# A planned order for sparse attention with a gated expert: ten instead of 21 products on zeros ahead of the first scores, and a newly searched order with other numbers in its planner

## The chip, the cores and the metric

The kernel runs on one core of a Trainium2 chip. The metric is the device time of one execution in microseconds (us). A core has a matrix engine (TensorE, PE in the profile, its weight loads PEld), three engines for elementwise work (VectorE or DVE, ScalarE or ACT, GpSimd or POOL), a queue that issues the loads and stores here (SyncE, SP), and 16 DMA engines that carry them.

## The reference

Four batches, eight heads, 768 positions, head width 64. Attention looks at a band of 31 positions around each query and at 24 block summaries (the maximum of 32 keys, the mean of 32 values); a gated two-layer network with a token shift follows.

```python
    k_sum = k.reshape(B, H, nb, block, D).max(axis=3)
    v_sum = v.reshape(B, H, nb, block, D).mean(axis=3)
    ...
    scores_l_m = np.where(mask_l, scores_l, -1000000000.0)
    scores_all = np.concatenate([scores_l_m, scores_s], axis=-1)
    ...
    a = a / (np.sum(a, axis=-1, keepdims=True) + 1e-09)
    return np.matmul(a, v_all).astype(np.float32)
    ...
    xk = mu_k * x + (1.0 - mu_k) * x_prev
    xr = mu_r * x + (1.0 - mu_r) * x_prev
    k = np.maximum(xk @ w_k, 0.0)
    v = k * k @ w_v
    r = 1.0 / (1.0 + np.exp(-(xr @ w_r)))
    return (r * v).astype(np.float32)
```

## The kernel before

**The work.** A set is one batch and one pair of heads (16 sets); a unit is one half of a set's positions (32 units). The keys of a set lie in a tile `kt` in 12 windows of 64 positions, each followed by 24 columns for the block maxima, which DVE reduces (L423 to L431, tiles `kg`, `ks`) and copies in (L435). The values of a unit lie in a tile `vx`, 120 rows for each window, of which 24 are block means: for the first batch PE makes these (L447, then L455), ACT takes them out of PSUM, and POOL or DVE spreads them (L461); for the others DVE sums blocks (L381), PE transposes them (L384), and a DMA broadcasts them into each `vx` tile (L468). A unit is a chain over four engines: scores on PE (L487, tile `sc`), mask and row minimum on DVE (L497), exponentials on ACT (L501), the reciprocal of their sums (L509), a normalization on ACT, DVE or POOL (L518, L512, L523), three transposes for each head on PE (L535), copies out of PSUM (L541 on ACT, L543 on DVE, tile `pts`), products with the values on PE (L550, tile `av`), and a copy to the features (L564, L565).

Each half batch of 384 positions then goes through the network. The shifted mixes of x (L583 to L596, or on PE with diagonal matrices, L614 to L620) are split into a high and a low part, so that three fast products replace an exact one. The gate is L637 to L639 and a sigmoid (L651), the first layer L666 with relu, square and split (L672 to L681), the second layer L691, and its last eighth L717, after which DVE multiplies by the gate (L723) and SP stores. The weights come as 64-bit words and are turned into 32-bit halves by DVE, ACT and POOL (L325 to L361) in the first 100 us.

**The order.** All these operations are recorded first, with what they read and write (`Plan.op`), and nothing is decided by arrival: `ORDER` is a list of operation numbers, some with a letter for the engine, and `Plan.schedule` walks through it. It gives each operation a start in a planned time from `LENGTH` (its duration), `SWITCH` (changes of kind on PE), `LATENCY` (from an engine to a waiting one), and the `DMA_` numbers, and hands out the buffers of each pool, the one that is free first. Then the instructions are emitted in that order, and every engine runs its own queue strictly in it. So the numbers don't act on the chip; what acts is the order, the buffer that each operation gets, and the number of products on zeros.

**Products on zeros.** Until the first gate product, each gap that the plan shows on PE is filled at L764 with products of a tile `still` of zeros, one for each `WARM` = 230 ns of planned gap. They run in PE's queue like any other instruction: what stands behind them waits for them.

The line numbers are those of this kernel; in the changed one they are one or two higher from L155 on.

## Time and profile before

| what | value |
|---|---|
| median of three timed runs | 452.86 us (451.57 to 452.99) |
| the profiled execution's own time | 453.34 us |
| its span, first to last instruction | 451.5 us |
| busy: PE, DVE, ACT, POOL | 443.9, 295.9, 284.2, 45.9 us |
| chain of waits: PE, DVE, ACT, DMA | 76%, 9%, 8%, 3% |
| products on zeros (L764) | 61 in the program, 122 rows of the trace |

A row of the timeline has the start, the time until the last instruction of the row ends, the engine, the line, the operation, the tiles as written<-read, their sizes and the count; in brackets the idle time ahead of it and what ended it. An exact product of 32-bit numbers is two rows on PE. A PE row's duration runs on beyond the start of the next one, since matmuls are pipelined; the time that PE spends on one is read from start to start. A wait is put down to what came last.

### The profile page before, as it was taken

The numbers are of one execution on the slowest core, as the hardware profiler recorded it, in microseconds if no ns is written. First come the engines' busy times: TensorE is split into PE (matmuls) and PEld (weight loads), VectorE is DVE, ScalarE is ACT, GpSimd is POOL, SyncE is SP. The second block draws the span as 40 slices with busy tenths as digits, with TensorE's granted clock in tenths as the row PEclk, the third lists the DMA queues.
The fourth block names the chain that finished last, engine by engine and source line by source line (L and its number), as shares of the span: only waits on it lengthen the run. The fifth ranks groups of instructions, "written<-read, shape, count | busy, mean of one in ns | idle before, by whom it ended". The sixth has DMA issues, their size and how long they took to land.

```text
span 451.5 us, 9681 instructions
## 1 busy us (share of the span) xinstructions
PE 443.9 (98%) x3608; PEld 381.6 (85%) x3608; DVE 295.9 (66%) x944; ACT 284.2 (63%) x843; POOL 45.9 (10%) x96
## 2 busy tenths in 40 slices
PE   9999999999999999999999999999999999999996
PEld 8867888789888789888988879888889888989985
DVE  2999999997887877828677676358364533445131
ACT  2889999987775849569574586466675434232211
POOL 0443222000230100000200001011002000000000
PEclk9999999999999999999999999999999999999999
DMA  8976684551557543240723112105100000003002
GB/s 311 403 262 221 208 326 131 179 208 33 145 169 217 220 132 91 85 147 1 221 73 120 53 56 84 43 19 177 48 2 0 2 0 1 0 1 116 1 0 93
DMA packets 26878, 51.95 MB, mean 115 GB/s; under 512 B 2512, under 2 KB 14416, under 8 KB 26832
## 3 DMA queue, kind: packets, MB, share of 16 engines
q1 hardware_dynamic: 26832, 51.35, 33.8%
q8 instruction: 28, 0.46, 0.4%
q14 instruction: 18, 0.15, 0.1%
HBM read 43.28 MB, written 6.29 MB: 110 GB/s over the span
## 4 chain that ended last, share of the span: by engine, by line
PE 76%; DVE 9%; ACT 8%; DMA 3%; issue 2%; SPq 1%; DVEq 0%; POOL 0%; POOLq 0%
PE mm L666 25%; PE mm L691 23%; PE av L550 4%; PE pt L535 4%; PE mm L637 4%; PE mm L639 4%; PE mm L638 4%; PE sc L487 4%; PE mm L717 3%; DMA kt<-in_k 2%; ACT y L501 2%; PE av L764 2%; DMA vx<-vm 1%; DVE y L497 1%; DVE we L336 1%
## 5 line engine op out<-in xcount | busy, mean ns | idle before, releaser
L666 PE MATMUL mm<-xs,wk_h 128*128 128x384 f32 x512 | 101.4, 340 | 0.0
L501 ACT ACTIVATE y<-y,mn 128x120 f32<-128x120 f32 x192 | 74.1, 388 | 30.5 <-DVE mn L497 30.1
L666 PEld LDWEIGHTS mm<-xs,wk_h 128*128 128x128 f32 x512 | 89.6, 188 | 3.7 <-ACT r L672 0.8
L691 PE MATMUL mm<-wv_h,kh 128*128 128x512 f32 x168 | 67.5, 402 | 0.0
L691 PE MATMUL mm<-wv_l,kh 128*128 128x512 f32 x168 | 66.3, 395 | 0.0
L497 DVE CUSTOM_DVE_ANT_0 y<-sc,fixed_sb 128x120 f32<-128x120 f32 x192 | 46.5, 276 | 25.5 <-PE pt L535 13.3
L666 PE MATMUL mm<-xs,wk_l 128*128 128x384 f32 x256 | 55.2, 337 | 0.0
L676 ACT ACTIVATE r<-r 128x384 f32<-128x384 f32 x64 | 32.9, 521 | 27.7 <-DVE r L674 27.2
L691 PE MATMUL mm<-wv_h,kl 128*128 128x512 f32 x168 | 49.1, 401 | 0.5 <-DVE kl L681 0.5
L681 DVE TENSOR_TENSOR kl<-r,kh 128x384 fp32r<-128x384 f32 x64 | 35.3, 556 | 19.1 <-ACT kh L680 11.1
L666 PEld LDWEIGHTS mm<-xs,wk_l 128*128 128x128 f32 x256 | 45.5, 188 | 0.0
L672 ACT ACTIVATE r<-mm 128x384 f32<-128x384 f32 x39 | 19.1, 489 | 38.8 <-PE mm L666 31.0
L590 DVE SCALAR_TENSOR_TENSOR xa<-vx,fixed_sb,xa 128x384 f32<-128x384 f32 x60 | 37.0, 622 | 9.1 <-ACT xa L583 7.4
L637 PE MATMUL mm<-wr_h,xs 128*128 128x512 f32 x96 | 39.0, 407 | 0.0
L639 PE MATMUL mm<-wr_h,xs 128*128 128x512 f32 x96 | 38.0, 396 | 0.0
L638 PE MATMUL mm<-wr_l,xs 128*128 128x512 f32 x96 | 37.9, 395 | 0.0
L596 DVE TENSOR_TENSOR xs<-xa,xs 128x384 fp32r<-128x384 f32 x60 | 33.0, 558 | 6.9 <-ACT xs L593 5.6
L691 PEld LDWEIGHTS mm<-wv_h,kh 128*128 128x128 f32 x168 | 31.6, 188 | 6.5 <-ACT kh L680 0.4
L691 PEld LDWEIGHTS mm<-wv_l,kh 128*128 128x128 f32 x168 | 31.6, 188 | 6.0
L501 ACT ACTIVATION_READ_ACCUMULATOR y<-y,mn 128x1 f32 x192 | 36.5, 190 | 0.0
L691 PEld LDWEIGHTS mm<-wv_h,kl 128*128 128x128 f32 x168 | 30.7, 188 | 6.8 <-DVE kl L681 0.9
L535 PE MATMUL pt<-fixed_sb,y 128*120 128x128 f32 x192 | 33.1, 281 | 0.1
(88 smaller groups left out, 699.2 us busy)
## 6 DMA issues: line engine op xcount, KB each, us to landing
vx<-in_v SPq DMA_DIRECT2D x32, 384.0 KB, 4.1
kt<-in_k SPq DMA_DIRECT2D x15, 544.0 KB, 4.9
qt<-in_q SPq DMA_DIRECT2D x32, 192.0 KB, 3.8
out<-z SPq DMA_DIRECT2D x23, 256.0 KB, 4.2
st<-in_vT SPq DMA_DIRECT2D x12, 384.0 KB, 4.5
st<-in_w_k SPq DMA_DIRECT2D x8, 512.0 KB
st<-in_w_v SPq DMA_DIRECT2D x8, 512.0 KB
st<-in_w_r SPq DMA_DIRECT2D x4, 512.0 KB, 8.0
```

The lines of the kernel that those rows point to most:

```text
L497: op("DVE", "mask", lambda h=h, i=i, var=var: nc.vector.tensor_tensor_reduce(out=y[h].t[:, i, :], in0=sc[h].t[:, i, 0:NK], in1=mask_sb[:, ...
L501: op("ACT", "exp", lambda h=h, i=i: nc.scalar.activation(y[h].t[:, i, :], y[h].t[:, i, :], AF.Exp, bias=mn[h].t[:, i:i + 1], scale=-1.0, a ...
L535: nc.tensor.transpose(out=pt.t[0:NK, i * P:(i + 1) * P], in_=y[h].t[:, i, :], identity=ident_sb)
L590: op("DVE", "mixd", lambda xt=xt, xa=xa, p=p: nc.vector.scalar_tensor_tensor(out=xa.t, in0=xt.t[:, 1 + lo:1 + lo + HT], scalar=mu_sb[:, wh ...
L596: op("DVE", "sub", lambda xa=xa, xh=xh, xl=xl: nc.vector.tensor_tensor(out=xl.t, in0=xa.t, in1=xh.t.bitcast(F32), op=ALU.subtract), reads= ...
L637: nc.tensor.matmul(ps[t].t, xh.t[:, ts], wr_h[:, p, :], start=(p == 0), stop=False)
L638: nc.tensor.matmul(ps[t].t, xh.t[:, ts], wr_l[:, p, :], start=False, stop=False)
L639: nc.tensor.matmul(ps[t].t, xl.t[:, ts], wr_h[:, p, :], start=False, stop=(p == NPAIR - 1))
L666: nc.tensor.matmul(ps.t[:, 0:HT], w[:, j, p, :], x[p][s].t, start=(n == 0), stop=(n == 11))
L676: op("ACT", "square", lambda: nc.scalar.activation(r.t, r.t, AF.Square), reads=[(r, 0)], writes=[(r, 0)])
L681: op("DVE", "sub", lambda: nc.vector.tensor_tensor(out=kl.t, in0=r.t, in1=kh.t.bitcast(F32), op=ALU.subtract), reads=[(r, 0), (kh, 0)], wr ...
L691: nc.tensor.matmul(acc[t].t, a.t[:, t * P:(t + 1) * P], w[:, j, :], start=start, stop=stop)
```

## The change

The diff does four things. The planner's numbers are replaced: other lengths on PE, other switches and latencies, and for loads of the later batches a later landing (`LATE`, twice that for keys) and for the broadcasts of block means four times the size and 480 ns more for the issue. `ORDER` is a new list. The products on zeros are counted from 1000 ns of planned time instead of 600 and at 430 ns each up to 6000 ns, 230 ns after that. The branch for `SPLIT` isn't taken in either kernel.

```diff
-    score=776, transpose=245, vtrans=82, vpool=800, vsel=75, values=848, mixe=1400, gate=2780, gate_p=2085, e1=2085,
-    e2a=1390, e2b=695, e2=695, e2h=350,
+    score=776, transpose=245, vtrans=30, vpool=800, vsel=320, values=848, mixe=1400, gate=2797, gate_p=2095, e1=2095,
+    e2a=1398, e2b=700, e2=700, e2h=350,
...
-SWITCH = dict(MS=100, SM=112, MV=108, VM=112, TM=85, ST=55, VT=55, TS=175, TV=175)
-LATENCY = dict(M=201, S=265, V=236, T=228, DVE=115, ACT=133, POOL=180, SP=0)
+SWITCH = dict(MS=100, SM=112, MV=108, TM=55, TS=175, TV=175)
+LATENCY = dict(M=201, S=130, V=120, T=300, DVE=115, ACT=133, POOL=180, SP=0)
...
-WARM = 230
+WARM, WARM_COLD, COLD = 230, 430, 6000
...
+LATE = 400
...
 ORDER = """
-252 227 17 18 204 0 10 39 52 21 229 32 22 23 24 25 20 19 205 59 41 40 206 212 1 210 208 216 213 207 5D 211 4D 12D 214
...
+17 18 204 0 10 39 52 21 229 22 23 32 20 19 24 25 252 205 59 40 41 1 216 214 208 206 8 212 217 7 207 12D 13 210 254 79
...
-                now[e] = start + DMA_ISSUE
+                now[e] = start + DMA_ISSUE + o.more[0]
                 dma = max(dma, start + DMA_START) + DMA_EACH + o.size / DMA_BYTES_PER_NS
-                o.finish = dma + DMA_END
+                o.finish = dma + DMA_END + o.more[1]
...
-               writes=[(vt, 0)], size=P * S * 4)
+               writes=[(vt, 0)], size=P * S * 4, more=(0, LATE))
...
-               writes=[(kt, f"k{n}")], size=P * (hi - lo) * 4)
+               writes=[(kt, f"k{n}")], size=P * (hi - lo) * 4, more=(0, 2 * LATE if b else 0))
...
-                   writes=[(vw[hf], x) for x in "abc"], size=P * HW * 512)
+                   writes=[(vw[hf], x) for x in "abc"], size=P * HW * 512, more=(0, LATE if b else 0))
...
-                   reads=[(means, 0)], writes=[(x, "b")], size=NS * HW * 512)
+                   reads=[(means, 0)], writes=[(x, "b")], size=4 * NS * HW * 512, more=(480, 0))
...
-           writes=[(qt, 0)], size=P * HT * 4)
+           writes=[(qt, 0)], size=P * HT * 4, more=(0, LATE if b else 0))
...
-    end, early = 600, True
+    end, early = 1000, True
     for o in order:
         if o.eng == "PE" and early:
-            for _ in range(int((o.start - end) // WARM)):
+            for _ in range(int(max(0, o.start - max(end, COLD)) // WARM + max(0, min(o.start, COLD) - end) // WARM_COLD)):
                 nc.tensor.matmul(spare, still, still, start=True, stop=True)
```

What the new list and the new buffers do is seen in the order of the instructions on each engine. First PE from its first instruction: products on zeros (from `still`), the scores of the first and second unit (from `kt_61` and `kt_62`), and the first transposes (from `y`). Before:

```order
L764 MATMUL av_146<-still 128x128 x21
L487 MATMUL sc_143<-kt_61,qt_65 64x120 x2
L487 MATMUL sc_144<-kt_61,qt_65 64x120 x2
...
L764 MATMUL av_146<-still 128x128 x25
L487 MATMUL sc_143<-kt_62,qt_66 64x120 x2
...
L535 MATMUL pt_145<-fixed_sb,y_89 120x128 x3
L764 MATMUL av_146<-still 128x128 x3
L535 MATMUL pt_145<-fixed_sb,y_90 120x128 x3
L764 MATMUL av_146<-still 128x128 x3
L447 MATMUL mm_147<-vx_71,fixed_sb 32x128 x2
```

And in the change:

```order
L766 MATMUL av_146<-still 128x128 x10
L489 MATMUL sc_143<-kt_61,qt_65 64x120 x2
L489 MATMUL sc_144<-kt_61,qt_65 64x120 x2
...
L766 MATMUL av_146<-still 128x128 x22
L489 MATMUL sc_144<-kt_62,qt_66 64x120 x2
...
L766 MATMUL av_146<-still 128x128 x4
L537 MATMUL pt_145<-fixed_sb,y_90 120x128 x3
L766 MATMUL av_146<-still 128x128 x6
L449 MATMUL mm_147<-vx_69,fixed_sb 32x128 x2
```

The products on zeros ahead of the first scores go from 21 to 10, those ahead of the second from 25 to 22; four new ones stand ahead of the first transposes, and of these those of the other head come first. The pooling of values (from `vx`, `fixed_sb`) moves ahead of the second three transposes. In all there are 50 instead of 61.

Next DVE, from the conversion of the first gate weights (`we`, `wc`, `wr_l`, from the staging tiles `st`) to the block maxima of the second set (`kg_79`, `ks_81`, copied into `kt_62`). Before:

```order
L336 SCALAR_TENSOR_TENSOR we_139<-st_136,we_139 128x512
L298 TENSOR_SCALAR diag_sb<-fixed_sb 128x128
L340 SCALAR_TENSOR_TENSOR wc_141<-wc_141,we_139 128x512
L509 RECIPROCAL rc_100<-sm_97 128x6
L427 TENSOR_REDUCE kg_79<-kt_62 128x1
L423 TENSOR_REDUCE kg_79<-kt_62 128x48
L431 TENSOR_TENSOR ks_81<-kg_79 128x24
L332 TENSOR_SCALAR we_140<-st_137 128x512
L435 COPY kt_62<-ks_81 128x12x24
L336 SCALAR_TENSOR_TENSOR we_140<-st_137,we_140 128x512
L361 TENSOR_TENSOR wr_l<-wc_141,wr_h 128x512
```

And in the change:

```order
L341 SCALAR_TENSOR_TENSOR wc_141<-wc_141,we_139 128x512
L425 TENSOR_REDUCE kg_79<-kt_62 128x48
L429 TENSOR_REDUCE kg_79<-kt_62 128x1
L433 TENSOR_TENSOR ks_81<-kg_79 128x24
L511 RECIPROCAL rc_100<-sm_97 128x6
L437 COPY kt_62<-ks_81 128x12x24
L333 TENSOR_SCALAR we_140<-st_137 128x512
L299 TENSOR_SCALAR diag_sb<-fixed_sb,om_sb 128x128
L362 TENSOR_TENSOR wr_l<-wc_141,wr_h 128x512
L299 TENSOR_SCALAR diag_sb<-fixed_sb,om_sb 128x128
L499 ISA y_91,mn_95<-sc_143,fixed_sb 128x120
```

The copy into `kt_62` now comes ahead of the second sign (`we_140`), the reduction ahead of the reciprocal, and the diagonals (`diag_sb`) come behind all of it.

Last PE at the second transpose of block sums (from `vs`). Before, with the end of the products with values ahead of it and the gate behind it:

```order
L550 MATMUL av_146<-pts_103,vx_73 64x64
L550 MATMUL av_146<-pts_104,vx_73 64x64
L384 MATMUL pt_145<-fixed_sb,vs_82 96x128
L637 MATMUL mm_147<-wr_h,xs_116 128x512
L638 MATMUL mm_147<-wr_l,xs_116 128x512
```

And in the change, with the gate's twelve products of one row of positions cut to their ends:

```order
L552 MATMUL av_146<-pts_103,vx_72 64x64
L552 MATMUL av_146<-pts_104,vx_72 64x64
L639 MATMUL mm_149<-wr_h,xs_114 128x512
...
L641 MATMUL mm_149<-wr_h,xs_121 128x512
L385 MATMUL pt_145<-fixed_sb,vs_82 96x128
L639 MATMUL mm_147<-wr_h,xs_114 128x512
L640 MATMUL mm_147<-wr_l,xs_114 128x512
```

The transpose of `vs` stands twelve gate products further back. Counted over the whole program, PE has the same products but those on zeros; DVE has 11 more relus (36, from 25) and 8 more copies of transposed weights (26, from 18), and POOL 12 fewer normalizing rows (18, from 30) and 8 fewer mixing rows (6, from 14).

## The prediction

> **What bounds the kernel now.** I read the page's first part, then the table of windows with cuts at the places where the program changes character, then the timeline of TensorE (PE) from the start, and at last the waits of PE.

> ```profile
> span 451.5 us, 9681 instructions
> PE 443.9 (98%) x3608; PEld 381.6 (85%) x3608; DVE 295.9 (66%) x944; ACT 284.2 (63%) x843; POOL 45.9 (10%) x96
> ...
> 0.00:10.00 10.00, 9.01 (x70) 8.73 (x71) 2.00 (x8) 1.28 (x1) 0.48 (x7) 1.00 0.83 298
> 10.00:24.80 14.80, 14.26 (x187) 12.50 (x185) 14.72 (x53) 12.56 (x49) 4.91 (x6) 1.00 1.03 402
> 24.80:64.00 39.20, 39.14 (x452) 30.94 (x452) 37.60 (x129) 38.17 (x122) 13.95 (x20) 1.00 0.72 242
> 64.00:105.00 41.00, 40.95 (x279) 34.23 (x278) 39.65 (x102) 38.44 (x105) 3.55 (x6) 1.00 0.49 171
> 105.00:165.00 60.00, 58.00 (x616) 49.23 (x616) 47.90 (x182) 40.80 (x152) 10.22 (x27) 1.00 0.48 153
> 165.00:447.60 282.60, 282.52 (x2014) 245.95 (x2012) 153.31 (x473) 152.95 (x417) 12.76 (x31) 1.00 0.19 59
> ```

> The windows' columns are the stretch, its length, the busy time of PE, of its weight loads, of VectorE (DVE), ScalarE (ACT) and GpSimd (POOL), the granted clock, the DMA share and GB/s. PE is busy without a break from 24.8 to 105 us (0.11 us idle in 80.2) and from 165 to 447.6 us (0.08 us). Its work there is the same set of products before and after, so a new order can't shorten it. What can change is what PE does before 24.8 us, where much of its busy time is products on zeros that fill waits, and the 2.0 us that it is idle between 105 and 165 us. The timeline of PE shows the first part:

> ```profile
> 0.99 7.85 PE L764 MATMUL av<-still 128*128 128x128 f32 x42 [0.99 <-POOL still L758]
> 8.78 0.85 PE L487 MATMUL sc<-kt,qt 64*64 64x120 f32 x24
> 9.55 5.85 PE L764 MATMUL av<-still 128*128 128x128 f32 x50
> 15.33 0.85 PE L487 MATMUL sc<-kt,qt 64*64 64x120 f32 x24
> ...
> 24.38 0.49 PE L764 MATMUL av<-still 128*128 128x128 f32 x2 [0.54 <-DVE vx L564]
> 24.80 0.40 PE L455 MATMUL mm<-sp,fixed_sb 128*24 128x128 f32 x2
> ```

> One product on zeros in the source is two rows of the trace (21 are x42). The first 42 take 7.79 us to the first scores (0.99 to 8.78), the next 50 take 5.78 us (9.55 to 15.33). Counted in windows of line L764 alone, the early ones are slow and the later ones fast:

> ```profile
> 1.00:4.00 3.00, 3.00 (x14) 3.00 (x15) 1.00 0.70 226
> 7.00:8.00 1.00, 1.00 (x10) 1.00 (x10) 1.00 1.02 406
> ```

> 14 in 3 us are 0.214 us a row, so 0.43 us a product while slow; 50 in 5.78 us are 0.231 us a product when fast. The column of the granted clock says 1.00 in both, so the pace is the better witness. The pace turns at about 7.0 us: 7.79 us for 42 rows is 28 rows at 0.214 and 14 at 0.128. That is 6.0 us after PE's first product.

> **Products ahead of the first scores: 21 become 10.** Were they what the first scores waited for? DVE says yes:

> ```profile
> 3.60 1.25 DVE L423 TENSOR_REDUCE kg<-kt 128x24 f32<-128x384 f32 x2 [3.60 <-DMA kt<-in_k]
> ...
> 5.17 0.31 DVE L435 COPY kt<-ks 128x288 f32<-128x288 f32 x1
> 9.68 0.28 DVE L497 CUSTOM_DVE_ANT_0 y<-sc,fixed_sb 128x120 f32<-128x120 f32 x1 [4.20 <-PE sc L487]
> ...
> 10.77 0.29 DVE L298 TENSOR_SCALAR diag_sb<-fixed_sb 128x128 f32<-128x128 f32 x1
> 10.97 0.28 DVE L298 TENSOR_SCALAR diag_sb<-fixed_sb,om_sb 128x128 f32<-128x128 f32 x1
> 11.17 0.42 DVE L332 TENSOR_SCALAR we<-st 128x512 f32<-128x512 f32 x1
> ...
> 14.93 0.30 DVE L435 COPY kt<-ks 128x288 f32<-128x288 f32 x1
> ```

> The keys were complete at 5.48 us and DVE stood idle for 4.20 us until the scores came. The other operand, the queries, is issued at 1.6 us and takes 4.5 us to land:

> ```profile
> L476 SPq DMA_DIRECT2D qt<-in_q x1: 432/432/432, 1.6 to 1.6; - x1
> ...
> DMA to landing us min/median/max: 4.5/4.5/4.5
> ```

> So the first scores can't start before about 6.2 us whatever PE does; the order of the first 25 loads is the same in both kernels. In the change ten products end at 0.99 + 20 x 0.214 and a little for the first, 5.4 us. PE then pauses for 0.9 us, a wait for the queries in place of the removed products, and the scores run from 6.3 us, 2.5 us earlier than 8.78. They take 0.77 us at the fast pace (8.78 to 9.55) and, scaled by 0.43/0.231, 1.4 us at the slow one.

> **What the pause does to the pace decides the rest.** Behind the first scores stand 22 products instead of 25, and the second scores are queued behind them on PE. If the pause changes nothing and the pace turns at 7.0 us, the scores end at 7.5 us and the 22 take 5.1 us: second scores at 12.6 us. If the 6.0 us are counted anew from 6.3 us, the pace turns at 12.3 us: scores to 7.7 us, 10.7 slow products, 11.3 fast ones, second scores at 14.9 us. Before, they started at 15.33 us, so the lead is 2.7 or 0.4 us. No row shows a pause ahead of the turn. I take the middle, 1.5 us, keep both ends, and treat each as a rival; what speaks for the middle is that the pause falls in the second half of the only run-up that the trace shows.

> [...]

> Are the second scores' operands there by then? From the first mask to the end of the copy of the keys' maxima DVE took 5.55 us (9.68 to 15.23). In the change three diagonals (0.20 us each from start to start), the second sign (0.42) and the coefficients (about 0.1) stand elsewhere, so some 4.4 us. With the first mask at 7.8 to 8.0 us the operands are ready at about 12.4 us: just in time for the fast end, early for the slow one. So the products set the lead, not the data.

> Between the second scores and row 24.80 the change has 18 products instead of 15 (+0.7 us), and the 0.54 us wait at 24.38 us should go, since what it waits for is DVE's, which is ahead too. **Term one: 1.5 - 0.7 + 0.5 = 1.3 us of lead at 24.8 us**, ends 0.2 and 2.5 us.

> **Does the lead last?** From 24.8 to 105 us PE never waits, but DVE is busy for 77.25 of 80.2 us and ACT for 76.61, so they only just keep ahead. They start about 1.8 us earlier too (7.9 against 9.68 us), which covers the lead. After 165 us they have half of their time free. I keep the lead whole.

> **The idle time between 105 and 165 us.** PE's timeline shows where it waited and what ended that, in brackets, and the chain of waits what lay behind (its last two rows):

> ```profile
> 123.66 0.92 PE L550 MATMUL av<-pts,vx 120*64 120x64 f32 x24 [0.40 <-DMA vx<-vm]
> ...
> 143.74 0.91 PE L550 MATMUL av<-pts,vx 120*64 120x64 f32 x22 [0.57 <-DVE pts L543]
> ...
> 147.79 0.96 PE L691 MATMUL mm<-wv_h,kl 128*128 128x512 f32 x3 [0.51 <-DVE kl L681]
> ...
> 160.78 0.31 PE L384 MATMUL pt<-fixed_sb,vs 128*96 128x128 f32 x1 [0.53 <-DVE vs L381]
> ...
> 119.23 4.38 DMA vx<-vm
> ...
> 136.09 5.21 DMA kt<-in_k
> ```

> These four are the whole 2.0 us. One is a broadcast of block means that lands 4.4 us after its issue; the next two, at 143 and 147 us, follow a load of keys that lands after 5.2 us and stops DVE; the last is the block sums of a later batch. The new numbers put all of these loads later in the plan (0.4 us, for keys 0.8 us, for the means four times the bytes), so the order leaves them more room; and on PE the second block-mean transpose stands twelve gate products (12 x 0.23 = 2.8 us) further back, five times its wait. In the place of these waits others can come late, since SP's queue of loads is in a new order too from its 26th load on, and each load there stands behind one that waits for a buffer. Bounds: all 2.0 us go, or 2.0 us stay. **Term two: 1.3 us**, nearer the first, since three of four have a cause that the numbers now contain.

> **Changes of kind on PE.** The order counts 29 instead of 17 steps from a 512- or 384-wide product to scores or values, and 1 instead of 14 from a transpose to these.

> ```profile
> 95.75 0.40 PE L639 MATMUL mm<-wr_h,xs 128*128 128x512 f32 x1
> 96.08 0.85 PE L487 MATMUL sc<-kt,qt 64*64 64x120 f32 x24
> 96.85 0.54 PE L535 MATMUL pt<-fixed_sb,y 128*120 128x128 f32 x3
> 97.15 1.63 PE L666 MATMUL mm<-xs,wk_h 128*128 128x384 f32 x8
> ...
> 122.00 0.49 PE L535 MATMUL pt<-fixed_sb,y 128*120 128x128 f32 x3
> 122.42 0.85 PE L487 MATMUL sc<-kt,qt 64*64 64x120 f32 x24
> ```

> A product ahead of scores holds PE 0.33 us instead of 0.23 (12 x 0.1 = +1.2 us); three transposes hold it 0.42 us ahead of scores and 0.30 us ahead of a product (13 x 0.12 = -1.5 us, of which the first product behind gives some back). I cost this at nothing. The tail behind 447.6 us has the same instructions.

> **The sum.** 1.3 + 1.3 = 2.6 us off the profiled execution, whose own time is 453.34 us: 450.7 us. That execution lies 0.48 us above the median of the three timed runs (452.86), so I forecast 450.3 us for the median.

> **Rivals.** A measurement of this kernel can tell about 0.3%, 1.36 us, from no change.
> First, the pace turns on time: the lead is 2.5 us, with term two 3.8 us, 449.1 us; with all of term two 448.4 us. For it speaks that the pause is short beside 6.0 us.
> Second, the 6.0 us start anew behind the pause: lead 0.2 us, total 1.5 us, 451.4 us.
> Third, the loads come late at other places and term two is nothing: 1.3 us, 451.6 us. For it speaks that a plan whose times were thought to fit left 2.0 us before.
> Fourth, the lead is hidden anyway: operands of a later step (values, the third scores) are as late as before, and PE waits where it ran products: 452.7 us. Against it: DVE is busy for 14.72 of 14.80 us up to 24.8 us, and starts earlier.
> Fifth, **slower: DVE becomes the bound between 24.8 and 105 us.** The groups give its means:

> ```profile
> L423 DVE TENSOR_REDUCE kg<-kt 128x48 f32<-128x768 f32 x15 | 14.1, 944 | 3.0 <-DMA kt<-in_k 3.0
> L512 DVE TENSOR_TENSOR y<-y,rc 128x360 f32<-128x360 f32 x29 | 15.1, 528 | 0.2
> L543 DVE COPY pts<-pt 120x384 f32<-120x384 f32 x18 | 10.0, 553 | 7.0 <-PE pt L535 7.0
> ```

> Up to its third multiplication by the gate (L723, the end of the first half batch) the order gives DVE 15 more rows: one more reduction of keys (0.94), two normalizations (1.06), two copies of transposed weights (1.11), four masks (0.20 each from start to start), and four casts, a relu and two small ones (some 2.4 by the means of their groups), less two evacuations, a spread of means, a diagonal and a sign (some 2.4): about 3.9 us. It starts 1.8 us earlier and has 2.95 us without work there. If the free time lies where it can't be used, DVE is 2.1 us late, the lead is lost and PE waits: 453.34 + 2.1, less 0.48, 455.0 us. It decides once the added work exceeds the earlier start by more than the usable free time. Against it: the masks and the reduction are for a later batch and nothing on PE needs them yet.

> **How the numbers follow.** Forecast 0.38, pace on time 0.24, pace anew 0.10, term two nothing 0.14, hidden 0.05, DVE bound 0.09. The range takes in the first four: 447.5 (all of both terms, with 0.9 us for the scatter of 1.4 us in the three runs) to 452.9 us. Faster by over 0.3% (under 451.5): nearly all of the forecast, all of the first rival, half of the next two, 0.72; slower by over 0.3% (above 454.2): 0.08; within it 0.20.

> **What would show it.** In the profile of the change: first scores at 6.3 us with a wait of some 0.9 us ahead of them on the queries; the rows of the 22 products turning from 0.214 to 0.116 us each near 7 or 10 or 12 us; second scores at 12.6 to 14.9 us; the second selection of block means (L455 before) at about 23.5 us; PE idle under 1 us between 105 and 165 us. Wrong would be first scores later than 7 us, a PE idle time over 2 us after 25 us, or waits of PE for DVE at 25 to 105 us.

## The result, and the profile after

| what | before | change |
|---|---|---|
| median | 452.39 us (451.57 to 452.99, four runs) | 449.19 us (448.20 to 449.64, four runs) |
| ratio to before, 95% interval | | 0.9928 (0.9908 to 0.9949) |
| profiled execution's own time, span | 453.34, 451.5 us | 448.20, 446.4 us |
| span behind the second selection of block means | 426.7 us | 424.5 us |

The change is faster by 3.2 us, 0.7%. The two profiled executions are 5.14 us apart, more than the medians: the one of before lies 0.95 us above its median, the one of the change 0.99 us below. Both matter for the reading below.

The page of the change has the same share of busy time on PE, and more work on DVE in place of POOL:

```profile
span 446.4 us, 9628 instructions
PE 439.6 (98%) x3586; PEld 376.1 (84%) x3586; DVE 302.0 (68%) x968; ACT 280.7 (63%) x840; POOL 33.3 (7%) x71
```

The windows of the change, with the same columns as before's and the last cut where PE's work ends now:

```profile
0.00:10.00 10.00, 7.83 (x72) 7.52 (x73) 4.12 (x19) 3.30 (x9) 0.44 (x6) 1.00 0.81 285
10.00:24.80 14.80, 14.18 (x198) 11.45 (x197) 13.63 (x54) 13.62 (x53) 5.02 (x8) 1.00 1.03 404
24.80:64.00 39.20, 39.02 (x430) 30.92 (x430) 38.20 (x127) 38.86 (x123) 10.98 (x19) 1.00 0.70 238
64.00:105.00 41.00, 41.00 (x309) 34.57 (x308) 39.67 (x103) 37.12 (x103) 4.40 (x7) 1.00 0.57 189
105.00:165.00 60.00, 60.00 (x608) 50.98 (x607) 51.04 (x197) 47.64 (x169) 3.80 (x9) 1.00 0.57 177
165.00:442.30 277.30, 277.30 (x1985) 240.66 (x1983) 154.60 (x473) 139.99 (x390) 8.64 (x24) 1.00 0.17 53
```

PE idles less from 105 to 165 us (58.00 busy before, 60.00 now), and 0.18 us from 24.8 to 105 us. The rest of the gain lies ahead of 24.8 us, as the timeline of PE in the change shows:

```profile
0.99 3.88 PE L766 MATMUL av<-still 128*128 128x128 f32 x20 [0.99 <-POOL vx L560]
6.04 0.85 PE L489 MATMUL sc<-kt,qt 64*64 64x120 f32 x24 [1.18 <-DMA qt<-in_q]
6.82 5.18 PE L766 MATMUL av<-still 128*128 128x128 f32 x44
12.62 0.85 PE L489 MATMUL sc<-kt,qt 64*64 64x120 f32 x24 [0.62 <-DVE kt L437]
...
21.56 0.39 PE L766 MATMUL av<-still 128*128 128x128 f32 x2
21.88 0.40 PE L457 MATMUL mm<-sp,fixed_sb 128*24 128x128 f32 x2
```

First scores at 6.04 instead of 8.78 us, second at 12.62 instead of 15.33, the second selection of block means at 21.88 instead of 24.80: 2.92 us of lead there. Two waits are new: 1.18 us for the queries and 0.62 us for the copy of the second keys' maxima, and the wait of 0.54 us ahead of the selection is gone. Behind this copy stands ACT, whose timeline begins late:

```profile
6.69 1.28 ACT L296 ACT_TABLE_LOAD   x1 [6.69 <-DMA fixed_sb<-in_fixed]
7.99 0.40 ACT L296 ACTIVATE diag_sb<-fixed_sb,om_sb 128x128 f32<-128x128 f32 x1
8.29 0.38 ACT L503 ACTIVATE y<-y,mn 128x120 f32<-128x120 f32 x1
```

In the new order a diagonal is ACT's first instruction. The load of the activation table stands ahead of it and began only when the constants were there, at 6.69 us. Before, an exponential came first on ACT, and the load began at 0.74 us (the timeline of ACT before):

```profile
0.74 1.28 ACT L501 ACT_TABLE_LOAD   x1 [0.74 <-PEq L860]
10.21 0.40 ACT L501 ACTIVATE y<-y,mn 128x120 f32<-128x120 f32 x1 [8.19 <-DVE mn L497]
```

The traces show what makes the difference. The diagonal waits for two things, the constants and DVE's `om_sb`. The diagonal itself carries one of these waits; the other, for the constants, stands in ACT's queue as an instruction of its own (an EVENT_SEMAPHORE of L296, at 6.64 us), and it stands ahead of the table load (6.69 us), which has no wait itself. The exponential has one wait, carries it itself, and so its 8.19 us came behind the load, which was done at 2.02 us. DVE, in its timeline, waits for the constants too, and later for ACT:

```profile
6.64 0.17 DVE L288 TENSOR_SCALAR om_sb<-fixed_sb 128x8 f32<-128x8 f32 x1 [1.31 <-DMA fixed_sb<-in_fixed]
6.95 0.28 DVE L499 CUSTOM_DVE_ANT_0 y<-sc,fixed_sb 128x120 f32<-128x120 f32 x1
...
12.19 0.19 DVE L511 RECIPROCAL rc<-sm 128x6 f32<-128x6 f32 x1 [0.27 <-ACT sm L508]
12.30 0.27 DVE L437 COPY kt<-ks 128x288 f32<-128x288 f32 x1
```

The copy that PE waits for ends at 12.57 us, 5.6 us behind the first mask, and the reciprocal ahead of it waited for ACT's sums.

### The profile page after: what moved, and what is told of

It reads as the page before. It is cut to its first block, busy times and chain, and to the rows that moved or that the text cites. A ratio compares the mean times of both kernels' runs of the same rounds, so it can differ in the third digit from the quotient of the medians.

```text
span 446.4 us, 9628 instructions
## 1 busy us (share of the span) xinstructions
PE 439.6 (98%) x3586; PEld 376.1 (84%) x3586; DVE 302.0 (68%) x968; ACT 280.7 (63%) x840; POOL 33.3 (7%) x71
## 4 chain that ended last, share of the span: by engine, by line
PE 88%; ACT 7%; DMA 2%; DVE 1%; issue 1%; SPq 0%; DVEq 0%; ACTq 0%
PE mm L668 29%; PE mm L693 26%; PE av L552 5%; PE pt L537 5%; PE mm L639 4%; PE mm L641 4%; PE mm L640 4%; PE sc L489 4%; PE mm L719 4%; ACT y L503 3%; DMA st<-in_w_k 1%; DMA fixed_sb<-in_fixed 1%; PE av L766 1%; ACT y L520 1%; ACT wc L326 1%
## 5 line engine op out<-in xcount | busy, mean ns | idle before, releaser
L676 DVE TENSOR_SCALAR r<-mm 128x384 f32<-128x384 f32 x36 | 20.0, 554 | 30.8 <-PE mm L668 30.7
L639 PE MATMUL mm<-wr_h,xs 128*128 128x512 f32 x96 | 38.9, 405 | 0.0
L503 ACT ACTIVATION_READ_ACCUMULATOR y<-y,mn 128x1 f32 x192 | 37.4, 195 | 0.0
L674 ACT ACTIVATE r<-mm 128x384 f32<-128x384 f32 x28 | 13.8, 493 | 30.4 <-PE mm L668 30.1
```

The costliest lines, as they stand in the source:

```text
L503: op("ACT", "exp", lambda h=h, i=i: nc.scalar.activation(y[h].t[:, i, :], y[h].t[:, i, :], AF.Exp, bias=mn[h].t[:, i:i + 1], scale=-1.0, a ...
L639: nc.tensor.matmul(ps[t].t, xh.t[:, ts], wr_h[:, p, :], start=(p == 0), stop=False)
```

## The experiments

Two questions were open: how much is due to the ten products and how much to the order, and what the lead meets next. Each version but two was timed beside the kernel before on the same chip (medians of before there: 452.38 us for before with 10 products, the change with 21, with the table loaded early, and with half the later products; 452.30 us for the change again and for the early table with fewer products; 452.18 us for the other four). The ratio is taken over all runs and differs by up to 0.0007 from that of the two medians. The table has what the profiles show in us: the time at which the pace of PE turns (from the trace's record of the granted clock), the starts of the first scores, the second scores and the second selection, and the span that is left behind this selection.

| version | median, ratio and interval | turn | first | second | selection | behind it |
|---|---|---|---|---|---|---|
| before | 452.39 | 7.10 | 8.78 | 15.33 | 24.80 | 426.7 |
| before, again | one run, 451.46 | 5.64 | 8.07 | 14.63 | 24.09 | 425.6 |
| before, one broadcast earlier | one run, 451.56 | 4.05 | 7.32 | 13.87 | 23.34 | 426.5 |
| before with 10 products | 449.97, 0.9935 (0.9916 to 0.9955) | 4.40 | 5.48 | 12.32 | 21.79 | 425.8 |
| change with 21 products | 450.02, 0.9946 (0.9929 to 0.9964) | 4.92 | 7.73 | 13.62 | 22.84 | 425.5 |
| change with no early products | 450.59, 0.9960 (0.9945 to 0.9976) | 10.00 | 5.59 | 13.52 | 22.74 | 426.1 |
| change | 449.19, 0.9928 (0.9908 to 0.9949) | 3.91 | 6.04 | 12.62 | 21.88 | 424.5 |
| change, again | 448.98, 0.9922 (0.9897 to 0.9947) | 6.69 | 5.56 | 12.34 | 21.59 | 424.5 |
| change, table loaded early | 448.20, 0.9902 (0.9884 to 0.9920) | 3.93 | 5.41 | 12.71 | 21.97 | 424.7 |
| change, half the later products | 448.60, 0.9912 (0.9895 to 0.9930) | 5.08 | 5.64 | 12.20 | 21.61 | 424.6 |
| change, early table, fewer products | 447.11, 0.9879 (0.9856 to 0.9901) | 7.04 | 5.65 | 12.12 | 21.04 | 424.7 |
| change, two copies twice on ACT | 449.78, 0.9952 (0.9935 to 0.9969) | 7.12 | 5.80 | 12.60 | 21.85 | 426.1 |
| change, relu first | 448.69, 0.9923 (0.9906 to 0.9940) | 4.45 | 5.67 | 12.66 | 21.91 | 425.4 |
| early table, fewer products, relu first | 447.33, 0.9897 (0.9878 to 0.9916) | 7.09 | 6.09 | 12.57 | 21.48 | 424.7 |

**The products by themselves, and the order by itself.** The gaps' counts of products on zeros were written into the program in place of the planner's arithmetic (`ZEROS` gives them in turn), in the order of the change with the old first count, and in the order of before with the new one:

```diff
+ZEROS = [21, 22, 4, 6, 1, 6, 1]      # the change: 10, 22, 4, 6, 1, 6, 1
...
+ZEROS = [10, 25, 3, 3, 2, 6, 1]      # before: 21, 25, 3, 3, 2, 6, 1
...
-            for _ in range(int((o.start - end) // WARM)):
+            for _ in range(ZEROS.pop(0) if int((o.start - end) // WARM) > 0 else 0):
```

> The changed kernel with 21 products on zeros ahead of the first scores again, all else as changed. If these products hold the scores and the lead lasts to the end: first scores at 7.2 to 8.8 us (by when the pace turns) instead of 6.04, second scores 1.2 to 2.7 us later, median 1.0 to 2.5 us over the changed kernel's 449.2, so 450.2 to 451.7 us. If the lead is hidden anyway by operands that are no earlier: 449.2 us, within 0.5.

> The kernel before with 10 products ahead of the first scores and its own order. If the products alone held the start: first scores at 6.1 us, second scores 1.2 to 2.7 us earlier than 15.33 unless the copy of the keys' maxima holds them, median 1.0 to 2.7 us under 452.4, so 449.7 to 451.4 us, with the 2.0 us of idle PE between 105 and 165 us still there. If the new order is needed to use the earlier scores: 452.4 us, within 0.5.

Each alone gives 2.4 us (452.38 less 450.02 and 449.97), and both together 3.2. The change with 21 products came out just under the 450.2 to 451.7 us expected, before with ten within its 449.7 to 451.4 us. So either is enough for most of the gain, and they overlap by 1.6 us. The timeline of PE in the change with 21 products, and in before's order with ten:

```profile
7.73 0.85 PE L489 MATMUL sc<-kt,qt 64*64 64x120 f32 x24
8.51 5.18 PE L766 MATMUL av<-still 128*128 128x128 f32 x44
13.62 0.85 PE L489 MATMUL sc<-kt,qt 64*64 64x120 f32 x24
...
61.84 1.65 PE L668 MATMUL mm<-xs,wk_h 128*128 128x384 f32 x8 [1.01 <-ACT r L674]
```

```profile
5.48 0.85 PE L487 MATMUL sc<-kt,qt 64*64 64x120 f32 x24 [0.37 <-DVE kt L435]
6.25 5.85 PE L764 MATMUL av<-still 128*128 128x128 f32 x50
12.32 0.85 PE L487 MATMUL sc<-kt,qt 64*64 64x120 f32 x24 [0.22 <-DVE kt L435]
```

With ten products in before's order the second scores come 2.3 us earlier than in the second profile of before (14.63), and 1.6 us earlier than in the profile of before's order whose pace turned nearest to theirs (13.87). In the order of the change the same cut brings them from 13.62 to 12.62 us only, since there they meet the copy of the keys' maxima. What the order does by itself ahead of 24.8 us is seen from the first scores to the second selection: 16.02 us in all three profiles of before's order with 21 products (8.78 to 24.80), 15.11 us with the new order and 21 products (7.73 to 22.84), though both have 40 products on zeros in between. 0.5 of these 0.9 us is the wait at 24.38 us that went. With the 0.6 to 0.7 us of idle time further on (below) this makes 1.6 us of the 2.4 that the order gains by itself; for the other 0.8 us the profiles show no place.

**Chance in the pace.** The first scores of before come at 7.32, 8.07 and 8.78 us where the pace turns at 4.05, 5.64 and 7.10 us: half a microsecond for each. With ten products they come at 5.41 to 6.09 us whatever the turn. The turn comes at 3.91 to 7.12 us in all thirteen profiles that begin with products at 0.99 us, with the pause and without. In five of the nine with ten products it comes ahead of the pause, which is long (1.2 us in the change) because the products have become fast and because the queries landed late in that execution. In two there is no pause to speak of, and in the last two a pause of 0.17 and 0.46 us ahead of the turn left it at 7.12 and 7.09 us, where before had it without one (7.10). So the count anew, of which the prediction was afraid, was not seen; a pause of 0.9 us ahead of the turn did not occur. What does move the turn was tried by leaving out the early products altogether:

```diff
-ZEROS = [10, 22, 4, 6, 1, 6, 1]
+ZEROS = [0, 22, 4, 6, 1, 6, 1]
```

> The change without its ten products ahead of the first scores; TensorE's first work is then the first scores. Theory A (the pace turns when one of freely running windows of about 3.4 us has been busy throughout, whatever the program does before): the first scores start at 5.5 to 6.1 us as before, at the slow pace (1.4 instead of 0.8 us), the pace turns between 9.0 and 12.8 us, the 22 products behind them end at 13.1 to 14.6 us instead of 12.0, so the second scores come 0.5 to 2 us later than in the change and the median is 449.6 to 451.2 us. Rival B (the turn is a matter of the time since the start of the program, and the early products have no part in it): turn at 3.9 to 7.1 us as in the nine profiles so far, second scores at 12.1 to 12.7 us, median within 0.5 us of the change, 448.7 to 449.5 us.

```profile
5.59 1.48 PE L489 MATMUL sc<-kt,qt 64*64 64x120 f32 x24 [5.59 <-DMA qt<-in_q]
6.99 6.60 PE L766 MATMUL av<-still 128*128 128x128 f32 x44
13.52 0.85 PE L489 MATMUL sc<-kt,qt 64*64 64x120 f32 x24
```

Theory A held against rival B: the scores take 1.40 us instead of 0.78 (5.59 to 6.99), the next 44 rows 6.60 instead of 5.18, the turn comes at 10.00 us, and the median is 1.4 and 1.6 us above the two measurements of the change. That is what the ten products that are left are worth; the eleven that went cost 0.8 to 1.0 us in this order (450.02 less 449.19 and 448.98).

The traces also show what went with the turn. In the record of the granted clock, which begins at the turn, every stretch of one speed between two changes lasts a whole multiple of 3.41 us: 128 to 131 of these windows at full speed from the turn on (130 in the first profiles of before and of the change, 443.73 us), and in the version with half the later products two at full speed, one at half and 126 at full. So in these profiles the clock changed only at the edge of a window, and where the edges lie differed from one execution to the next: the window that ends with the turn begins at 0.50 us in the first profile of the change and at 3.28 us in the second. In all fourteen profiles the window that ends with the turn held at least 2.92 us of PE's work, and a window ahead of it at most 2.71 us. These are the two nearest cases (windows of PE in the change, and in the change with two copies twice, which turned at 7.12 us):

```profile
0.50:3.91 3.41, 2.92 (x13) 1.00 0.62 189
0.29:3.70 3.41, 2.71 (x12) 1.00 0.54 172
```

"Busy throughout", as theory A has it, was not needed: 2.92 of 3.41 us sufficed. Of these two, the early turn has products from 0.49 us into their first window on, the late one from 0.70 us on. The pause of 0.46 us left 2.95 us of work in its window and did no harm. A pause of 0.9 us would leave 2.5 us (3.41 less 0.9), under the 2.71 us that didn't do; that it would cost one more window is an estimate from these numbers, and no run shows it.

**The table load.** The diagonal (8 in the list of operation numbers) was moved behind the first exponential on ACT (217), and separately half of the products on zeros behind the first scores were left out:

```diff
-206 8 212 217 7
+206 212 217 8 7
...
+ZEROS = [10, 11, 2, 3, 0, 3, 0]
```

> The changed kernel with one diagonal moved behind the first exponential on ACT, so that the load of the activation table no longer stands behind the wait for the constants. Theory: table load at 0.7 us instead of 6.69, first exponential at 7.2 instead of 8.29, sums of the first unit 0.6 to 1.1 us earlier, second scores up to 0.6 us earlier where the 22 products are done by then: median 0 to 0.6 us under the changed kernel. Rival, the products hold the second scores in most runs: no difference over 0.2 us.

> The changed kernel with 10, 11, 2, 3, 0, 3, 0 products instead of 10, 22, 4, 6, 1, 6, 1. If the products behind the first scores hold PE in runs where the pace turns late, and the pace doesn't fall back in the pauses: second scores at 12.6 us in every run, steps behind them earlier by up to 2 us, median 0.4 to 1.5 us under the changed kernel. Rival, the pauses of 2 us and more put PE back to the slow pace: rows of scores and transposes at twice the time in the first 25 us, median 0 to 2 us over it.

Both medians are below both measurements of the change, by 0.4 to 1.0 us, but the intervals overlap its own. The first gained more than the 0 to 0.6 us expected, and its profile shows no gain, because the constants landed a microsecond later in that execution (the timeline of DVE):

```profile
7.67 0.17 DVE L288 TENSOR_SCALAR om_sb<-fixed_sb 128x8 f32<-128x8 f32 x1 [2.34 <-DMA fixed_sb<-in_fixed]
7.75 0.28 DVE L499 CUSTOM_DVE_ANT_0 y<-sc,fixed_sb 128x120 f32<-128x120 f32 x1
```

In the change this wait ended at 6.64 us. So with the scores ready at 6.2 us it is the load of the constants that starts the chain. With half of the later products, PE pauses for 3.06 us, and the clock goes back:

```profile
6.42 2.72 PE L766 MATMUL av<-still 128*128 128x128 f32 x22
12.20 1.48 PE L489 MATMUL sc<-kt,qt 64*64 64x120 f32 x24 [3.06 <-DVE kt L437]
```

```profile
8.90:11.90 3.00, 0.24 (x3) 1.00 1.03 414
11.90:15.30 3.40, 3.10 (x32) 0.50 1.03 411
15.30:18.70 3.40, 3.10 (x42) 1.00 1.03 405
```

In these windows of PE the third column from the right is the granted clock: half speed from 11.9 to 15.3 us. The second scores took 1.41 us (12.20 to 13.61) instead of 0.78, and yet the second selection came at 21.61 us, no later than in the change (21.88), since fewer products stood ahead of it. The two edits together, with fewer products taken out so that the pauses stay short, are the fastest version:

```diff
-206 8 212 217 7
+206 212 217 8 7
...
+ZEROS = [10, 16, 2, 3, 1, 3, 1]
```

> The changed kernel with the table load early (one diagonal behind the first exponential) and 10, 16, 2, 3, 1, 3, 1 products. Theory: ACT's chain from the first mask to 60 us sets the time, and the early table takes up to 1.1 us out of it; fewer products keep PE from being late where its pace turns late. Median 447.2 to 448.4 us, 0.8 to 1.8 us under the changed kernel beside it. Rival: the pauses cost as much as the products did (one window of slow pace after 3 us of pause), no better than 448.2 of the early table alone.

> The changed kernel again, unaltered, for a second profile and for times beside the next kernel. If the turn of PE's pace is a matter of chance (3.91 us after the span's start in its first profile, 7.10 in that of the kernel before), it turns elsewhere this time, anywhere from 4.4 less to about 11 us; a turn behind 7.7 us would delay the second scores to 13 us and more. If the start of the scores decides and not the turn, the median is 449.2 within 0.4 us whatever the turn is.

The median of this version is 447.11 us, 5.2 us less than before and 1.9 us less than the change beside it (448.98 us; the ends of the two intervals just touch). The change's pace turned at 6.69 us this time, its second scores came at 12.34 us, and its median stayed within 0.4 us of 449.2, as expected if the turn is chance and the start of the scores decides. A turn as late as the 11 us of that expectation is not shown: with products from 0.99 us on, 7.12 us was the latest. The timelines of ACT and PE:

```profile
0.73 1.28 ACT L503 ACT_TABLE_LOAD   x1 [0.73 <-PEq L862]
7.51 0.40 ACT L503 ACTIVATE y<-y,mn 128x120 f32<-128x120 f32 x1 [5.50 <-DVE mn L499]
```

```profile
12.12 0.85 PE L489 MATMUL sc<-kt,qt 64*64 64x120 f32 x24 [1.22 <-DVE kt L437]
...
21.04 0.40 PE L457 MATMUL mm<-sp,fixed_sb 128*24 128x128 f32 x2
```

In the fastest version the first exponential runs at 7.51 instead of 8.29 us, though the first mask is 0.2 us later (7.18), the copy of the keys' maxima ends 4.9 us behind that mask instead of 5.6, and the selection comes 0.84 us earlier than in the change. The pause of 1.22 us did not bring the clock down.

**The idle time between 105 and 165 us.** Was the wait for the broadcast at 123 us due to its place in SP's queue? In before's order it (674 in the list) was moved ahead of the load of keys in front of it (1053), beside a second profile of before:

```diff
-... 1053 ... 674 ...
+... 674 1053 ...
```

> The kernel before with one broadcast of block means (the one that PE waited for at 123 us) moved two places ahead in SP's queue, ahead of a load of keys that waits 10 us for its buffer. If that wait is the queue's doing: no wait of PE for this broadcast, and the rest as it was, so 0.4 us less before 124 us; the waits at 143, 147 and 160 us stay or move. If the broadcast is late for another reason (its means, the transfer): the wait stays at 0.3 to 0.5 us.

> The kernel before, unaltered, for a second profile. If the turn of the pace is a matter of chance and the products hold the scores: with a turn at t us, first scores at 8.8 us less 0.46 for each us that t is under 7.1 (7.3 at 4 us), and the execution's time shorter by about as much than 453.34. If the turn is fixed by the work: 7.1 us again and 453.3 us.

The wait at 123 us was absent in both, so this tells nothing of the queue. But the second profile tells that the first was an unusual one. Its row of the windows, and the waits of PE (us in total, times, longest) that fall into it:

```profile
105.00:165.00 60.00, 59.28 (x625) 50.54 (x624) 49.66 (x189) 41.75 (x152) 10.10 (x27) 1.00 0.49 162
```

```profile
PE pt L384 <- DVE vs L381: 0.5, 1, 0.5
...
PE mm L691 <- DVE kl L681: 0.2, 1, 0.2
```

PE idles 0.72 us there instead of 2.00. The other two kernels with before's order idle 0.59 and 0.60 us there; elsewhere the one waits 1.1 us at 175 us (for a copy by ACT), the other 0.8 us at 71 us (for converted weights). The wait for the broadcast came once more, 0.31 us at 121 us with ten products. The ten with the new order idle 0.00 to 0.03 us there, but for one (0.62, below). What comes back in every profile of before's order, with 0.3 to 0.5 us, is the wait for `vs`, the block sums, whose transpose the new order moved twelve products back.

**What the lead meets next: ACT.** At 60 us PE waits for a relu in all seven profiles with the order of the change where nothing near it was edited. The timelines of ACT and PE in the change:

```profile
57.92 1.28 ACT L503 ACT_TABLE_LOAD   x1
59.22 0.40 ACT L503 ACTIVATE y<-y,mn 128x120 f32<-128x120 f32 x1
...
59.61 0.47 ACT L674 ACTIVATE r<-mm 128x384 f32<-128x384 f32 x1
```

```profile
60.13 1.67 PE L668 MATMUL mm<-xs,wk_h 128*128 128x384 f32 x8 [0.17 <-ACT r L674]
```

With 21 products that row stands at 61.84 us behind a wait of 1.01 us: its first scores are 1.69 us later, its selection only 0.96, this row 1.71. That fits a queue of ACT that carries the delay up to 60 us (in the change ACT is busy for 38.86 of the 39.20 us from 24.8 to 64 us). Two tests: two copies of weight words (L326) were written twice, and the relu was exchanged with the exponential ahead of it, which needs the table load.

```diff
-            nc.scalar.activation(wc.t.bitcast(F32), words()[0].bitcast(F32), AF.Copy, scale=2.0**-112)
+            for _ in range(SCALED.append(1) or 1 + (len(SCALED) in (3, 4))): nc.scalar.activation(...)
...
-365 441
+441 365
```

> The change with two of the ScalarE copies of weight words (0.58 us each from start to start) written twice: the ones that stood at 32.8 and 45.1 us. Theory A (from the first masks to 60 us ScalarE's queue is full, and its last link, the relu that TensorE waits for at 60 us, sets how much of the lead is left): that wait grows from 0.2 us to 1.0 to 1.4 us, and the median rises by 0.8 to 1.2 us, to 450.0 to 450.4. Rival B (ScalarE has room behind 24.8 us, the wait at 60 us comes from where the relu stands behind a table load): the wait stays under 0.5 us and the median within 0.4 us of the change.

> The change with two neighbours on ScalarE exchanged: the relu of the second product of the first layer ahead of the exponential that needs a table load of 1.28 us. Theory A (TensorE's wait at 60 us is for this relu, and nothing is as late right behind it): the wait of 0.2 to 0.5 us at 60 us is gone and the median falls by 0.2 to 0.5 us, to 448.6 to 449.0. Rival B (the lead meets the next link of ScalarE's queue, the scores' exponentials being 0.4 us later): a wait of the same size stands within the next 10 us and the median is within 0.2 us of the change.

> The same exchange in the version with the diagonal behind the first exponential and with fewer products on zeros behind the first scores (447.11 us in its own five rounds). Theory A: 0.3 us less, 446.6 to 447.0. Rival B: the same as without the exchange, 446.9 to 447.4.

With the added copies the relu runs at 60.75 instead of 59.61 us, and PE's row behind it 1.14 us later too (61.27 instead of 60.13), though the selection was as early as in the change (21.85). PE's wait falls at another place than expected (the timeline of PE):

```profile
52.65 0.54 PE L537 MATMUL pt<-fixed_sb,y 128*120 128x128 f32 x3 [0.72 <-ACT pts L543]
```

The median rose by 0.6 us against the first measurement of the change and 0.8 against the second. Against before beside it, it lies 2.4 us lower where the change lies 3.2 and 3.3 us lower, so by this it lost 0.8 to 0.9 us: the low end of the 0.8 to 1.2 expected, and more than the 0.4 that the rival allowed. The intervals overlap the change's. The trace is the firmer witness: the 1.16 us added to ACT ahead of 47 us, PE has lost by 60 us. That it is the relu that counts was wrong; a copy on ACT took its place. The exchange took the wait at 60 us away in both versions, but no gain is shown: 448.69 us lies in the 448.6 to 449.0 expected, but the ratio to before beside it, 0.9923, is that of the change (0.9928, 0.9922), and 447.33 us is no better than 447.11. In the first of the two a broadcast came late at 105 us (the timeline of PE):

```profile
105.62 0.92 PE L552 MATMUL av<-pts,vx 120*64 120x64 f32 x24 [0.64 <-DMA vx<-vm]
```

Whether the 0.2 to 0.4 us at 60 us are worth anything stays open; they are less than the scatter of one kernel's runs, of which the causes seen are the constants' landing (6.5 to 7.7 us) and single late broadcasts (PE waited 0.31 to 0.64 us for one).

## Why the prediction was right, and where it was not

450.3 us was predicted and 449.19 measured, inside the range of 447.5 to 452.9 us. The mechanism was the one named, with two parts: a lead at 24.8 us and less idle time from 105 to 165 us.

- **First scores.** Predicted at 6.3 us behind a wait of 0.9 us for the queries: 6.04 us, 1.18 us. The time was near, the working less so. The floor of about 6.2 us "whatever PE does" does not hold: with ten products or none the first scores started at 5.41 to 6.09 us. And the wait was 1.18 us because the pace turned before the ten products were done (4.87 us, not 5.4); where it turned later the wait was 0 to 0.46 us.
- **The pause and the pace.** This step failed. The middle of two cases was taken, a turn at 7.0 us and one counted anew from the pause to 12.3 us. In the change's profile the turn came at 3.91 us, ahead of the pause, so neither case occurred; in the others with ten products a pause ahead of the turn was at most 0.46 us, and the turn came at 7.09 us with it and at 7.10 without. The turn is a matter of chance within 3.2 us (3.91 to 7.12 us; 3.91 and 6.69 for the change, 7.10 and 5.64 for before), and the 7.1 us of the profile before was the late end of it. So the first rival was nearer here, with second scores at 12.6 us (12.62 measured). That its time, 449.1 us, is the one measured is luck in part: its term two is twice what the other profiles give, and it starts from a median 0.5 us too high. That a pause of 0.9 us ahead of the turn puts the turn off, by the count of 6.0 us or otherwise, no run here shows; what the runs showed in place of that count is the window of 3.41 us with 2.92 us of work or more in it.
- **"So the products set the lead, not the data."** Wrong by a little: in eight of the ten profiles of versions of the change the second scores wait for the copy of the keys' maxima, here 0.62 us. Its 4.4 us from the first mask to the end of this copy became 5.6. The table load is what it left out: the stretch is 4.6 us with 21 products, where the load was done before the first mask, 4.9 us in the three versions with the early table, and 5.2 to 5.8 us in the six others. That a diagonal came first on ACT was to be seen in the order.
- **Term one**, 1.3 us, measured 2.92 us in the profiled pair and 2.50 us between the second profiles (24.09 and 21.59). The +0.7 for 18 instead of 15 products and the -0.5 for the wait came out as -0.2 together (9.47 us from the second scores to the selection, now 9.26).
- **The lead lasts.** Right: PE idles 0.18 us from 24.8 to 105 us. DVE never became the bound, so the fifth rival fell, with a first mask 2.7 us earlier and not 1.8; it is ACT that stands just behind PE at 50 to 60 us.
- **Term two**, 1.3 us, measured 2.00 us in the profiled pair, but 0.6 to 0.7 us against the three other profiles of before's order. The 2.0 us from which it was sized belonged to one execution: three of its four waits did not come back or shrank.
- **Changes of kind**, costed at nothing: PE's work in the windows and its idle time account for all but 0.2 us of the 5.14 us (2.92 + 2.00), so they are small, as put.
- **From the profiled execution to the median.** 0.48 us was taken off; in the larger sample it is 0.95. Both terms were 2.3 us short of the pair of profiles, and the pair overstates the medians by 1.9 us (0.95 above, 0.99 below). Most of this cancelled; the forecast missed by 1.1 us, 0.6 of it from here and 0.5 because before's median is 452.39 in the larger sample and not 452.86.
- **The fourth rival's time**, 452.7 us, does not follow from its terms: without the lead and with term two it would be 452.86 less 1.3, 451.6 us.

What the 3.2 us between the medians consist of can be put together from the profiles. At the second selection the three profiles of before's order with 21 products stand at 24.08 us on the mean, and the four whose program is the change's up to there (the change twice, two copies twice, relu first) at 21.81: 2.3 us earlier. That is the lead of the first scores alone (8.06 and 5.77 us): the 0.9 us that the order saves with 21 products goes here into the wait of 0.2 to 1.0 us for the keys' maxima and what follows from it. With the 0.6 to 0.7 us behind 105 us it makes 2.9 to 3.0 of the 3.2 us. This sum is argued from single profiles, not shown term by term.

## What to carry to other kernels

Work that fills a wait on an in-order queue must end before what it waits for lands (21 products held the first scores here to 7.32 us and later, with ten they began at 5.41 to 6.09 us); its count is best fixed from the slow pace that TensorE started with here (0.214 us a row against 0.116), since the turn to the fast pace came by chance (3.91 to 7.12 us), but leaving it out altogether delayed that turn (to 10.00 us). Take the profile of before twice before sizing a term by its small waits, since of the four here three did not come back or shrank. Look for what an engine does first: a wait of its own, which the first instruction had here because it waits for two things, stood ahead of the table load and held it to 6.69 us. An instruction with one wait, here the critical exponential itself, belongs first (load at 0.73 us).
